# Two attention matmuls of a pair issued together, and the dense matmuls of both shares behind them

## The chip, the core and the metric

The kernel runs on one core of a Trainium2 chip. The core has a matrix engine (TensorE, PE in the profile, with its weight loads as PEld), a vector engine (VectorE, DVE), an activation engine (ScalarE, ACT), GpSimd (POOL), and a queue engine (SyncE, SP) that issues all the kernel's transfers. The metric is the device time of one execution in microseconds; the smaller the better.

## The reference

Two branches work on the same x (2048 rows, 512 columns, fp32) and are mixed by a gate per row:

```python
g = _sigmoid((x * gate_w).sum(-1, keepdims=True))
# A: a 2-D Fourier transform written as matrix products, real part only
a = x @ Wd_re.T;  b = x @ Wd_im.T
y = Ws_re @ a - Ws_im @ b
# B: attention with 32 heads of 16 columns, each query sees itself and the 255 keys before it
q, k, v = split(x @ wqkv)
p = softmax(where(mask, q @ k.T * 16 ** -0.5, -1e9))
o = (p @ v) @ wo
return g * y + (1 - g) * o
```

Inputs are fp32. The kernel keeps that precision by splitting each operand into a high and a low part and taking three products (hi*hi, hi*lo, lo*hi).

## The kernel before

**Attention.** The 32 heads are four groups (NG) of four pairs (NP) of two heads. Keys and queries are taken in 32 blocks of 64 (NB). A step n is one group and one block, 128 steps in all (N), and each step has four pairs p. For each pair there are two score matmuls:

- S, in `s_pair` (matmul at L319): 64 queries of two heads, zero-padded to a 128-wide stationary operand (`PAD[0, n]`), against a window of up to 320 keys in `ring[1]`. VectorE adds the mask and takes the row extreme (L321, which reads the bank), ScalarE takes the exp and the row sum (L324, which reads SBUF). S gives the maxima and sums only.
- T, in `t_pair` (matmul at L384): 64 keys of two heads (`PAD[1, n]`) against up to 320 queries in `ring[0]`, which gives the scores transposed. The row maxima are extra contraction rows of `ring[0]`, brought there by `m_rows` (L331 to L335 and two transfers). ScalarE takes the exp straight out of the bank (L385), GpSimd cuts the two corners of the window (L390, L394).

`pv` (L411) multiplies the transposed probabilities with v, for two steps at a time, on every odd step behind the third pair. T runs LAG = 18 steps behind S, so step n issues the S of block n and the T of block k = n - 18. Steps 0 to 17 have S alone, steps 18 to 127 both, steps 128 to 145 T alone. `make_pad` (L302 on ScalarE, L304 on VectorE) makes the padded operands of the next step behind pair 0.

**Banks.** S, T and the small transposes of `m_rows` and `l_rows` share one pool of four PSUM banks (`ps_a`), `pv` has two, the dense matmuls have two (`ps_d`).

**Dense work.** Everything else that TensorE does, all with 512 columns, is one generator, `dense()`: the projections for q, k (L238), v and the hidden transform (L260), then the transform along the sequence (L442), then the output (L604). Its `yield` stands behind every matmul. `fill(n)` takes matmuls from it by a quota, half a pair's rate at each call: 3.0 a pair before step 18, then 3.5, and 3.6 once the projections are done (`FILL_FIRST`, `FILL_PROJ`, `FILL_SEQ`). What is left of the generator when the loop ends runs alone.

**Who decides the order.** TensorE's instructions stay in the order of the program text. Those of VectorE, ScalarE and SP are placed by a scheduler when the kernel is built, so moving a line on TensorE can change the order in those queues as well. Each engine then works through its queue in that order.

The profile's L80 to L90 are the helpers that split an operand or a result into its high and low part, L55 the helper that issues a transfer.

Of the kernel before, what the change touches and what calls it, by code (L numbers as in the profile page):

```python
# [31 lines left out]
def fnet_window_mix(ctx: ExitStack, tc: tile.TileContext, xT, x, wqk, wv, wr, wi, cr, ci, wo, gw, out):  # L32
# [36 lines left out]
    @contextmanager  # L69
    def behind(*engines):  # L70
        with ExitStack() as es:
            for e in engines:
                if e in last:
                    es.enter_context(tc.issue_after(last[e]))
            yield
# [92 lines left out]
    def clear_rows(i, ss):  # L168
        nc.gpsimd.memset(f(ring[i][96:128, :, ss * 512:(ss + 1) * 512]), 0.0)
# [7 lines left out]
    def clear_pads():  # L177
        for t in vpad:
            nc.gpsimd.memset(t, 0.0)
        for t in pads[1]:  # L180
            nc.gpsimd.memset(f(t[96:128]), 1.0)
            for h in range(2):
                a = t[96:128, :, 64 * h:64 * h + 64]
                nc.vector.tensor_scalar(a, f(a), mrow[96:128, h:h + 1], None, op0=OP.mult)
# [108 lines left out]
    def make_pad(i, n):  # L293
        if not 0 <= n < NG * NB:
            return
        t = pads[i][n % NPAD]
        b = n % NB
        with behind(*(("act", "dve") if n < NPAD else ())):
            for h in range(2):
                src, dst = f(ring[i][:96, :, b * BQ:(b + 1) * BQ]), t[:96, :, 64 * h:64 * h + 64]  # L300
                if i and h:
                    nc.scalar.activation(dst, src, AF.Copy, scale=half[:96, h:h + 1])  # L302
                else:
                    nc.vector.tensor_scalar(dst, src, half[:96, h:h + 1], None, op0=OP.mult)  # L304
        PAD[i, n] = t
# [3 lines left out]
    def s_pair(n, p):  # L309
        j = n % NB  # L310
        u, jj = divmod(n, 8)
        if jj == 0 and p == 0:
            ML[u] = [at.tile([P, NP * 8], F32, name="nm"), at.tile([P, NP * 8], F32, name="l")]
        nm, l = ML[u]
        k0 = max(0, (j - 4) * BQ)
        w = (j + 1) * BQ - k0
        c = slice(p * 8 + jj, p * 8 + jj + 1)
        ps = ps_a.tile([P, 512], F32, name="s", tag="st")
        nc.tensor.matmul(ps[:, :w], PAD[0, n][:, p], ring[1][:, p, k0:k0 + w], start=True, stop=True)  # L319
        sm = at.tile([P, WIN], F32, name="sm", bufs=3)  # L320
        mark("dve", nc.vector.tensor_tensor_reduce(out=sm[:, :w], in0=ps[:, :w], in1=mask[:, WIN - w:],  # L321
                                                   scale=1.0, scalar=3e38, op0=OP.add, op1=OP.min,
                                                   accum_out=nm[:, c]))
        mark("act", nc.scalar.activation(sm[:, :w], sm[:, :w], AF.Exp, bias=nm[:, c], scale=-1.0,  # L324
                                         accum_out=l[:, c]))
# [31 lines left out]
    def v_load(n):  # L357
        if n >= NG * NB:
            return
        g, kb = divmod(n, NB)  # L360
        raw = at.tile([P, 4, 64], F32, name="vr")
        for h in range(2):
            ld(raw[64 * h:64 * h + 64].rearrange("r (c j) x -> r c j x", j=2),
               v_scr[kb // 4][:, :, h, g, :].rearrange("c (j r) x -> r c j x", r=64))
        VR[n] = raw

    def v_spread(n):
        if n >= NG * NB:
            return
        raw = VR.pop(n)  # L370
        v2 = vpad[n // 4 % 2]
        for h in range(2):
            r = slice(64 * h, 64 * h + 64)
            nc.gpsimd.tensor_copy(v2[r, :, :, 16 * h:16 * h + 16], raw[r].rearrange("r j (p d) -> r j p d", d=16))
        V2[n // 4] = v2

    def t_pair(n, p):
        q0 = n % NB * BQ
        w = min(WIN, S - q0)
        if p == 0:  # L380
            PT[n] = at.tile([P, NP, WIN], F32, name="pt", bufs=3)
        pt = PT[n]
        ps = ps_a.tile([P, 512], F32, name="t", tag="st")
        nc.tensor.matmul(ps[:, :w], PAD[1, n][:, p], ring[0][:, p, q0:q0 + w], start=True, stop=True)  # L384
        nc.scalar.activation(pt[:, p, :w], ps[:, :w], AF.Exp, scale=-1.0)  # L385
        if p % 2:
            ph = slice(p - 1, p + 1)
            for h in (0, 64):
                a = pt[h:h + 64, ph, 0:64]
                nc.gpsimd.affine_select(a, a, pattern=[[0, 2], [1, 64]], compare_op=OP.is_ge, fill=0.0,  # L390
                                        base=0, channel_multiplier=-1)
                if w == WIN:
                    a = pt[h:h + 64, ph, 256:320]
                    nc.gpsimd.affine_select(a, a, pattern=[[0, 2], [-1, 64]], compare_op=OP.is_gt, fill=0.0,  # L394
                                            base=0, channel_multiplier=1)

    def pv(n):
        g, kb = divmod(n, NB)
        v2 = V2[n // 4][:, n % 4]
        pt = PT.pop(n)  # L400
        q0 = kb * BQ
        w = min(WIN, S - q0)
        q = q0
        while q < q0 + w:
            sb = q // 512
            e = min(q0 + w, (sb + 1) * 512)
            first = (g, sb) not in OT
            if first:
                OT[g, sb] = ps_o.tile([P, 512], F32, name="o")
            for p in range(NP):  # L410
                nc.tensor.matmul(OT[g, sb][32 * p:32 * p + 32, q - sb * 512:e - sb * 512], v2[:, p],  # L411
                                 pt[:, p, q - q0:e - q0], start=first, stop=kb == 8 * sb + 7,
                                 skip_group_check=True)
            q = e
        if kb % 8 == 7:
            sb = kb // 8
            ps = OT.pop((g, sb))
            rl = at.tile([P, 512], F32, name="rl", bufs=1)
            ls = l_scr[g * 4 + sb]
            ld(rl, bass.AP(tensor=ls.tensor, offset=ls.offset, ap=[[512, 2 * NP], [0, 16], [1, 512]]))  # L420
            nc.vector.tensor_mul(rl, ps, rl)
            ld(o_scr[sb][g], rl)
# [190 lines left out]
    def need(key):  # L613
        while key not in have:
            next(stream)
# [3 lines left out]
    def ring_ahead(n):  # L619
        nonlocal loaded  # L620
        while loaded < 16:
            g, ss = divmod(loaded, 4)
            if n >= 32 * g + 8 * ss:
                need(("qk", g, ss))
            if ("qk", g, ss) not in have or n - LAG < 32 * (g - 1) + 8 * ss + 9:
                break
            with behind(*(("sp",) if g == 0 else ())):
                ring_load(g, ss)
            loaded += 1

    def fill(n):
        nonlocal quota
        rate = FILL_FIRST if n < LAG else FILL_SEQ if "proj" in have else FILL_PROJ
        quota += rate / 2
        while quota >= 1:
            next(stream, None)
            quota -= 1
# [7 lines left out]
    for n in range(N + LAG + 2):  # L645
        if n in (1, 3, 5):
            for i in range(2):
                clear_rows(1 - i, (n + 1) // 2)
        if n == 7:
            clear_pads()  # L650
        k = n - LAG
        ring_ahead(n + 1)
        if -4 <= k < N - 4 and k % 4 == 0:
            for c in range(2):
                need(("v", (k + 4) % NB // 2 + c))
            with behind(*(("sp",) if k < 4 else ())):
                v_load(k + 4)
        if -4 <= k and k % 4 == 2:
            v_spread(k + 2)
        if n == 0:  # L660
            make_pad(0, 0)
        if k == 0:
            make_pad(1, 0)
        for p in range(NP):
            if n < N:
                s_pair(n, p)
            fill(n)
            if 0 <= k < N:
                t_pair(k, p)
            if p == 0:  # L670
                make_pad(0, n + 1)
                if k >= 0:
                    make_pad(1, k + 1)
            fill(n)
            if p == 2 and n % 2:
                for j in (k - 2, k - 1):
                    if 0 <= j < N:
                        pv(j)
                if n % 8 == 1 and 1 < n <= N + 1:
                    m_rows(n // 8 - 1)  # L680
                    l_rows(n // 8 - 1)
# [47 lines left out]
```

## Time and profile before

| | us |
|---|---|
| median of 3 runs | 880.83 |
| lowest and highest run | 879.98, 882.15 |
| the profiled execution, its own time | 881.33 |
| its span | 879.5 |
| TensorE busy in the span | 866.5 |
| VectorE busy | 600.1 |
| ScalarE busy | 585.3 |
| GpSimd busy | 385.0 |

The span is the time from the first to the last instruction that the profiler recorded. Busy time of TensorE counts overlapping matmuls once. The first S and T that stand in one step start at 95.87 and 99.02, the last S at 668.6, the last T at 751.9; what follows is dense work and the output.

### The profile page before, as it was taken

The page shows a single profiled execution, that of the slowest core. Times are in us where ns is not written, and L with a number is a line of the kernel's source. Part 1 is how long each engine was busy: PE and PEld are TensorE (multiplying, and loading weights), DVE is VectorE, ACT ScalarE, POOL GpSimd, SP SyncE. Part 2 cuts the span into 40 slices and gives each one's busy share as a digit, 9 for nine tenths or more (in the row PEclk, how much of TensorE's full clock was granted, in tenths as well). Part 3 has the DMA queues.
Part 4 walks back from the last instruction along what each step waited for, and adds up shares of the span by engine and source line. Part 5 has one row for each costly group of instructions (what it writes and reads, how often), then busy time and mean ns, then how long its engine had stood idle before and what let it go on. Part 6 is the DMA issues. An engine that isn't in the chain of part 4 may idle for free.

```text
span 879.5 us, 17216 instructions
## 1 busy us (share of the span) xinstructions
PE 866.5 (99%) x5184; PEld 692.2 (79%) x5184; DVE 600.1 (68%) x1965; ACT 585.3 (67%) x1794; POOL 385.0 (44%) x1069
## 2 busy tenths in 40 slices
PE   7999899999999999999999999999999999999997
PEld 6888678777877878787778787877878777788885
DVE  4688788777887677777777777778776443454342
ACT  5488788889888887888878878888776444100010
POOL 9100165555544447564455566545656664000000
PEclk9999899999999999999999999999999999999999
DMA  7877668775766136543544353579643323455452
GB/s 265 261 228 214 198 205 272 233 237 174 221 207 210 45 99 200 147 138 120 175 131 140 127 148 115 143 230 348 211 143 126 130 92 126 137 174 156 149 159 88
DMA packets 89823, 152.13 MB, mean 173 GB/s; under 512 B 26753, under 2 KB 35457, under 8 KB 89729
## 3 DMA queue, kind: packets, MB, share of 16 engines
q1 hardware_dynamic: 89728, 151.02, 55.0%
q8 instruction: 41, 0.67, 0.3%
q14 instruction: 54, 0.43, 0.2%
HBM read 103.81 MB, written 47.19 MB: 172 GB/s over the span
## 4 chain that ended last, share of the span: by engine, by line
PE 98%; DMA 1%; ACT 1%; issue 0%; DVE 0%; SPq 0%; ACTq 0%
PE dc L442 41%; PE dab L260 10%; PE dqk L238 10%; PE s L319 9%; PE o L411 8%; PE t L384 8%; PE dv L260 5%; PE t L604 5%; PE s L226 1%; DMA ev<-o_scr 1%; PE s L343 0%; PE s L331 0%; DMA pt<-xT 0%; ACT sm L324 0%; ACT raw L80 0%
## 5 line engine op out<-in xcount | busy, mean ns | idle before, releaser
L442 PE MATMUL dc<-big,hi 128*128 128x512 f32 x1024 | 354.9, 395 | 0.0
L390 POOL TENSOR_SCALAR_AFFINE_SELECT pt<-pt 64x128 f32<-64x128 f32 x512 | 192.7, 376 | 292.1 <-ACT pt L385 276.2
L324 ACT ACTIVATE sm<-sm,nm 128x320 f32<-128x320 f32 (+4 forms) x512 | 276.8, 542 | 59.4 <-DVE nm L321 56.7
L321 DVE CUSTOM_DVE_ANT_0 sm<-s,mask 128x320 f32<-128x320 f32 (+4 forms) x512 | 232.3, 462 | 118.3 <-PE s L319 94.0
L385 ACT ACTIVATE pt<-t 128x320 f32<-128x320 f32 (+4 forms) x512 | 208.0, 412 | 81.3 <-PE t L384 78.7
L442 PEld LDWEIGHTS dc<-big,hi 128*128 128x128 f32 x1024 | 186.8, 188 | 28.0 <-issue 1.5
L442 PE MATMUL dc<-big,lo 128*128 128x512 f32 x512 | 202.6, 396 | 0.0
L319 PE MATMUL s<-ring,pad 128*128 128x320 f32 (+4 forms) x512 | 160.7, 314 | 0.0
L394 POOL TENSOR_SCALAR_AFFINE_SELECT pt<-pt 64x128 f32<-64x128 f32 x448 | 160.3, 358 | 0.0
L384 PE MATMUL t<-ring,pad 128*128 128x320 f32 (+4 forms) x512 | 154.8, 302 | 3.0 <-ACT pad L302 2.6
L304 DVE TENSOR_SCALAR pad<-ring,half 96x256 fp32r<-96x256 f32 x384 | 121.8, 359 | 19.7 <-PE t L384 19.2
L319 PEld LDWEIGHTS s<-ring,pad 128*128 128x128 f32 x512 | 96.4, 188 | 38.7 <-issue 9.3
L384 PEld LDWEIGHTS t<-ring,pad 128*128 128x128 f32 x512 | 96.5, 189 | 20.3 <-ACT pad L302 2.9
L442 PEld LDWEIGHTS dc<-big,lo 128*128 128x128 f32 x512 | 96.2, 188 | 16.5 <-issue 1.6
L83 DVE TENSOR_TENSOR lo<-raw,hi 128x512 fp32r<-128x512 f32 x146 | 100.0, 711 | 0.3 <-ACT hi L80 0.3
L324 ACT ACTIVATION_READ_ACCUMULATOR sm<-sm,nm 128x1 f32 x512 | 98.1, 192 | 0.0
L82 DVE CAST hi<-raw 128x512 fp32r<-128x512 f32 x142 | 56.8, 437 | 51.8 <-PE dc L442 31.8
L260 PE MATMUL dab<-hi,big 128*128 128x512 f32 x256 | 91.1, 396 | 0.0
L238 PE MATMUL dqk<-big,hi 128*128 128x512 f32 x240 | 87.3, 399 | 0.0
L80 ACT CAST raw<-ev 128x512 fp32r<-128x512 f32 x16 | 9.9, 622 | 110.0 <-DVE lo L83 72.3
L411 PE MATMUL o<-pt,vpad 128*32 128x320 f32 (+4 forms) x1408 | 78.6, 352 | 0.0
L411 PEld LDWEIGHTS o<-pt,vpad 128*32 128x32 f32 x1408 | 36.0, 109 | 36.9 <-issue 19.8
(79 smaller groups left out, 823.1 us busy)
## 6 DMA issues: line engine op xcount, KB each, us to landing
qk_scr<-hl SPq DMA_DIRECT2D x32, 512.0 KB
ring<-qk_scr SPq DMA_DIRECT2D x32, 512.0 KB
raw<-cr SPq DMA_DIRECT2D x32, 512.0 KB
raw<-ci SPq DMA_DIRECT2D x32, 512.0 KB
ab_scr<-hl SPq DMA_DIRECT2D x20, 512.0 KB
big<-ab_scr SPq DMA_DIRECT2D x20, 512.0 KB
ring<-qk_scr SPq DMA_DIRECT2D x32, 256.0 KB
r_scr<-ev SPq DMA_DIRECT2D x25, 256.0 KB
```

What stands on the lines that cost most here:

```text
L238: nc.tensor.matmul(ps, w[a][:, c:c + 128], XT[dk, ss][:, b], start=n == 0, stop=n == 11)
L260: nc.tensor.matmul(ps, XT[dk, ss][:, a, c * 128:(c + 1) * 128], wh[b], start=n == 0, stop=n == 11)
L304: nc.vector.tensor_scalar(dst, src, half[:96, h:h + 1], None, op0=OP.mult)
L319: nc.tensor.matmul(ps[:, :w], PAD[0, n][:, p], ring[1][:, p, k0:k0 + w], start=True, stop=True)
L321: mark("dve", nc.vector.tensor_tensor_reduce(out=sm[:, :w], in0=ps[:, :w], in1=mask[:, WIN - w:], scale=1.0, scalar=3e38, op0=OP.add, op1= ...
L324: mark("act", nc.scalar.activation(sm[:, :w], sm[:, :w], AF.Exp, bias=nm[:, c], scale=-1.0, accum_out=l[:, c]))
L384: nc.tensor.matmul(ps[:, :w], PAD[1, n][:, p], ring[0][:, p, q0:q0 + w], start=True, stop=True)
L385: nc.scalar.activation(pt[:, p, :w], ps[:, :w], AF.Exp, scale=-1.0)
L390: nc.gpsimd.affine_select(a, a, pattern=[[0, 2], [1, 64]], compare_op=OP.is_ge, fill=0.0, base=0, channel_multiplier=-1)
L394: nc.gpsimd.affine_select(a, a, pattern=[[0, 2], [-1, 64]], compare_op=OP.is_gt, fill=0.0, base=0, channel_multiplier=1)
L411: nc.tensor.matmul(OT[g, sb][32 * p:32 * p + 32, q - sb * 512:e - sb * 512], v2[:, p], pt[:, p, q - q0:e - q0], start=first, stop=kb == 8 ...
L442: nc.tensor.matmul(ps, w[a][:, s8 * 128:(s8 + 1) * 128], ab[SC[i]][:, b], start=i == 0 and a + b == 0, stop=i == 15 and a == 1)
```

## The change

In each pair the call `fill(n)` that stood between `s_pair` and `t_pair` moves behind `t_pair`. T of a pair is then issued directly behind S, and the two shares of dense matmuls stand behind them in one run; behind pair 0 the calls of `make_pad` stand between the two shares, as before.

```diff
--- before
+++ after
@@ -664,9 +664,9 @@
         for p in range(NP):
             if n < N:
                 s_pair(n, p)
-            fill(n)
             if 0 <= k < N:
                 t_pair(k, p)
+            fill(n)
             if p == 0:
                 make_pad(0, n + 1)
                 if k >= 0:
```

## The prediction

> **What bounds the kernel now.** I read the page first: engines, then the chain that ended last.
>
> ```profile
> PE 866.5 (99%) x5184; PEld 692.2 (79%) x5184; DVE 600.1 (68%) x1965; ACT 585.3 (67%) x1794; POOL 385.0 (44%) x1069
> PE 98%; DMA 1%; ACT 1%; issue 0%; DVE 0%; SPq 0%; ACTq 0%
> ```
>
> TensorE is the bound: 98% of the chain is its own work, so a reordering can only pay or cost through (a) the pace of the matmul stream and (b) TensorE's waits. For (b) the list of TensorE's waits has two entries that concern T:
>
> ```profile
> PE t L384 <- ACT pad L302: 2.6, 1, 2.6
> PE t L384 <- ACT pt L385: 0.4, 1, 0.4
> ```
>
> One long and one short wait in 512 T. For (a) the timeline in the middle of the attention loop:
>
> ```profile
> 306.56 0.31 PE L319 MATMUL s<-ring,pad 128*128 128x320 f32 x1
> 306.70 0.39 PE L260 MATMUL dab<-hi,big 128*128 128x512 f32 x1
> 306.93 0.31 PE L384 MATMUL t<-ring,pad 128*128 128x320 f32 x1
> 307.08 0.39 PE L260 MATMUL dab<-lo,big 128*128 128x512 f32 x1
> ```
>
> Columns: start in us, length, engine, line, operation. Lengths overlap; what counts is start to start. S (L319) is followed after 0.14 to 0.15 us, a dense matmul after 0.23, T (L384) after 0.15. Over all rows the medians are 147 ns behind a 320-column S, 147 behind such a T, 227 to 233 behind 512 columns. It makes no difference what follows: dense to dense has a median of 228 to 230, dense to S or T 229 to 231.
>
> **Part 1: the matmul stream.** Per pair the order S, 1 or 2 dense, T, 1 or 2 dense becomes S, T, 2 to 4 dense. The quota is added twice in both, so by the end of each pair the same dense matmuls have been issued (some 3.5 a pair), and the built order shows the same totals. S and T stand together in the 110 steps that have both: 440 pairs. Before step 18 there is no T and after step 127 no S; nothing changes there.
>
> The only new neighbourhood is T directly behind S. No row shows it, so I bound it by what T's weight load needs. Each weight load takes 188 ns in the record (PEld), longer than the 147 ns of the S that would cover it. How much must really be covered is shown where a matmul is very short:
>
> ```profile
> 426.70 0.19 PE L384 MATMUL t<-ring,pad 128*128 128x64 f32 x1
> 426.70 0.19 PEld L442 LDWEIGHTS dc<-big,hi 128*128 128x128 f32 x1
> 426.73 0.47 PE L442 MATMUL dc<-big,hi 128*128 128x512 f32 x1
> 427.04 0.40 PE L442 MATMUL dc<-big,lo 128*128 128x512 f32 x1
> ```
>
> The load starts with the 64-column T; the dense matmul behind it frees the array at 427.04, and less its usual 0.23 it had its weights at 426.81: about 0.11 us after the load began. So a load is hidden behind any matmul of 0.11 us or more, and S holds the array for 0.147. It already hides the load of a dense matmul, of the same 128x128 shape, 397 times. Estimate for T behind S: 147 ns, as now: sum 0. [...] The narrow S and T at the ends of a group expose the rest of a load before and after alike.
>
> [...]
>
> **Part 2: the first T.** At step 18 TensorE waits for the first T's padded operand:
>
> ```profile
> 95.87 0.31 PE L319 MATMUL s<-ring,pad 128*128 128x320 f32 x1
> 96.02 0.40 PE L238 MATMUL dqk<-big,hi 128*128 128x512 f32 x1
> 98.58 0.34 DVE L304 TENSOR_SCALAR pad<-ring,half 96x256 fp32r<-96x256 f32 x1
> 99.02 0.60 PE L384 MATMUL t<-ring,pad 128*128 128x320 f32 x1 [2.60 <-ACT pad L302]
> ```
>
> The table of stretches puts the granted clock at 0.50 from 98.25 to 105.07; the page's 0.97 of 50:150 is this. ScalarE's pads were done at 98.32, so what came last is VectorE's pad, at 98.92. In the built order the instructions ahead of that pad on VectorE are the same as before, and they need only the S of 95.87 and earlier matmuls. T therefore still starts at 99.0, but the one dense matmul that ran inside the gap is now behind T. Queued behind the waiting T is the whole matmul stream, and with it the evictions. Cost: one dense matmul that was free: +0.23 us at full clock, 0.43 at half if the half-clock stretch grew with it. I take 0.23, since the stretch ends at a time of its own.
>
> **Part 3: the banks.** S and T share four banks; VectorE (L321) frees S's, ScalarE (L385) frees T's. T is asked for 0.40 us earlier on average (the one or two dense matmuls it overtakes). Rhythm and distance between T's stay; the question is whether ScalarE's exp follows. I went through the timeline's T rows: from the exp of the T two pairs back to a T's start the median is 1.32 us, and 23 of 510 have under 0.5. If every exp stayed where it is in time while its T moved up, 16 T would wait, 1.3 us together. If it all moved up with T, 0. ScalarE has room: it waited for T 78.7 us in 119 waits, which an earlier T shortens; in the built order an exp of T no longer stands behind the exp of its own S (121 of 440 did, 1 does). In between I take half: +0.65 us. VectorE's order changes in places (an eviction ahead of an S), but S keeps its place; for its banks I take nothing, the cover being ScalarE's and VectorE's idle fifth; uncovered it is the second rival's kind of cost.
>
> The one recorded wait of a T for a bank:
>
> ```profile
> 177.27 0.60 ACT L86 ACTIVATE hl<-dab 128x512 fp32r<-128x512 f32 x1 [1.54 <-PE dab L260]
> 177.76 0.34 ACT L324 ACTIVATE sm<-sm,nm 128x64 f32<-128x64 f32 x1
> 178.09 0.42 ACT L385 ACTIVATE pt<-t 128x320 f32<-128x320 f32 x1
> 178.57 0.41 PE L384 MATMUL t<-ring,pad 128*128 128x320 f32 x1 [0.39 <-ACT pt L385]
> ```
>
> ScalarE works in order: an eviction that waited (its matmul was long done, so for its store's buffer) held up the exp. In the built order this exp stands ahead of the 0.34 us one: -0.2 us.
>
> **What else moves.** The pads for the next step are issued behind the first T; those after the first have 2.2 us and mostly 8 to 10 on ScalarE. GpSimd's order is unchanged and its input comes earlier. On SP some ring loads now stand ahead of the small row stores (l_scr, m_scr); those rows are read five steps, some 22 us, later. Sum 0. The final phase (745 us on) is untouched.
>
> **Sum.** +0.23 +0.65 -0.2 = +0.7 us on the profiled execution's 881.33 (span 879.5 and 1.8 around it): 882.0. That execution lies 0.5 above the median of the three runs, 880.83; against the median the forecast is 881.5. About 0.3%, 2.6 us, is what a measurement of this kernel can tell from no change, so this is "same".
>
> **Rivals.**
> - *ScalarE's exp comes later relative to where it was (slower).* If the exps slip by 0.1 us behind their present times while T is asked for 0.40 earlier, the shortfalls over the same rows add to 3.4 us; by 0.2, to 5.9. From about 0.07 on it is a measurable loss. For: ScalarE is 80 to 86% busy in 150 to 650. Against: its 78.7 us of waiting for T. At 0.1 that is 880.83+0.23-0.2+3.4 = 884.3. Chance 0.18.
> - *One new wait that halves the clock (slower).* The wait at 99.0 cost 2.8 us and then 6.83 us at clock 0.50, that is 3.4: 6.2 in all. One more, say a T behind a late pad or eviction, gives 880.8+6.2 = 887.0. Against: the longest other wait of a T in the trace is 0.39. Chance 0.08. [...]
> - *T's weight load is not hidden behind S (slower).* [...] Against: the 64-column row above. Chance 0.03.
> - *The waits shrink (faster).* The half-clock stretch is two stretches of 3.41; if it were one, -1.7 us; with the late starts of T outside the first (1.4 us in all, from the rows) gone, -3.1: 877.7. For: where the gap falls against those stretches may vary. Against: the gap gets longer. Chance 0.10.
> - *The edit does nothing in the stream* can be left out: the built order has the 440 adjacent pairs.
>
> **How the numbers follow.** Forecast (same): 0.61. Slower 0.18+0.08+0.03 = 0.29; faster 0.10. Range: down to 878.6, the lowest run (879.98) less the 1.4 us of small T waits; up to 886, which takes in the exp rival up to a slip of some 0.17 us and leaves out the two dearer ones.
>
> **What would show it.** Right: S to T 147 ns, TensorE still 98% of the chain, the first T again at 99.0 with a gap of 3.0 and half clock behind it, T waits for banks under 2 us. Wrong: S to T of 180 or more; many short waits "PE t <- ACT pt"; a second half-clock stretch.

## The result and the profile after

The changed kernel takes 882.54 us (median of 21 runs, 881.37 to 884.02), the kernel before 880.86 beside it (21 runs, 878.96 to 882.35). The ratio is 1.0018, 95% interval 1.0012 to 1.0024: 1.6 us slower, 1.1 to 2.1. This lies within the 0.3% that the prediction counted as "no change", but it is not zero. The profiled execution took 882.81 with a span of 881.0, that is 1.5 more than the profiled execution before.

From the page of the kernel after, busy time by engine and the chain by engine:

```profile
PE 867.3 (98%) x5184; PEld 690.6 (78%) x5184; DVE 604.8 (69%) x1965; ACT 590.3 (67%) x1794; POOL 384.9 (44%) x1069
PE 93%; DVE 2%; DMA 2%; ACT 1%; issue 0%; SPq 0%; ACTq 0%
```

TensorE's busy time has hardly moved (867.3 us against 866.5 before), yet its share of the chain fell from 98% to 93%: the chain now leaves TensorE for VectorE, ScalarE and transfers. The list of TensorE's waits (engine, operation, what it waited for; total us, times, longest) shows where:

```profile
PE t L384 <- ACT pad L302: 2.8, 1, 2.8
PE s L319 <- ACT pt L385: 0.8, 2, 0.6
PE t L384 <- ACT pt L385: 0.7, 2, 0.4
PE t L384 <- DVE nm L321: 0.2, 1, 0.2
PE dab L260 <- DVE hl L88: 0.2, 1, 0.2
```

One long wait as before, but T, S and a dense matmul now wait for banks: for VectorE's row extreme (`nm`, L321), for ScalarE's exp (`pt`, L385), for an eviction (`hl`, L88). The list holds the longer waits only; late starts of 0.05 to 0.15 us are found by going through the rows. The timeline of TensorE in the middle of the loop (start, length, engine, line, operation):

```profile
304.27 0.31 PE L319 MATMUL s<-ring,pad 128*128 128x320 f32 x1
304.43 0.31 PE L384 MATMUL t<-ring,pad 128*128 128x320 f32 x1
```

T starts 0.16 us behind S in this row, and over all rows the median from S to T is 147 ns: T's weight load, 0.19 us from 304.28 on in the row, is hidden behind S. Around the first T the timeline after reads:

```profile
96.23 0.31 PE L319 MATMUL s<-ring,pad 128*128 128x320 f32 x1
98.94 0.34 DVE L304 TENSOR_SCALAR pad<-ring,half 96x256 fp32r<-96x256 f32 x1
99.38 0.38 PE L384 MATMUL t<-ring,pad 128*128 128x320 f32 x1 [2.84 <-ACT pad L302]
99.60 0.39 PE L238 MATMUL dqk<-big,hi 128*128 128x512 f32 x1
```

T starts 3.15 us behind its S, as before (95.87 to 99.02), with the dense matmul now behind it instead of in the gap. Half clock follows, but shorter here; the table of stretches (window, its length, busy us of PE, PEld, DVE, ACT and POOL with counts, granted clock, DMA share, GB/s):

```profile
98.00:102.00 4.00, 2.62 (x10) 2.23 (x11) 2.97 (x8) 2.10 (x7) 0.55 (x2) 0.81 0.54 167
102.00:106.00 4.00, 4.00 (x17) 3.44 (x16) 1.99 (x8) 2.49 (x7) 1.45 (x5) 0.77 0.99 221
```

At half clock for x us of a 4 us window the mean is 1 - x/8; 0.81 and 0.77 give 1.5 and 1.8, together about 3.4 us; a window from 100.45 to 103.87 has 0.50. Before, it was 6.8. The same kernel profiled again had 6.8 (below), so this length is not fixed by the order, and the 1.7 us between the two is no work of the change.

The granted clock that is on record for each run says more. It is a mean over the span, rounded to 0.001. It is 1.000, hardly any half clock, in 28 of 80 runs of the kernel before (on four chips), but in 1 of 33 runs of the changed one. So half clock has become more frequent; that the longer gap is the reason is likely, not shown. It does not make up the difference: where the clock is 0.999 or more the changed kernel is 1.3 us slower in the means (33 and 7 runs), at 0.997 and 0.998 1.4 (36 and 16), below that 1.6 (11 and 10). Nor does a run get longer by all that half clock takes: the kernel before has means of 880.5, 881.2 and 880.9 in these three classes. What takes it up the record doesn't show.

A bank wait in full, all engines, after:

```profile
169.62 0.68 DVE L90 SCALAR_TENSOR_TENSOR hl<-dab,hl 128x512 fp32r<-128x512 f32 x1
170.22 0.47 DVE L321 CUSTOM_DVE_ANT_0 sm<-s,mask 128x320 f32<-128x320 f32 x1
170.24 0.31 PE L319 MATMUL s<-ring,pad 128*128 128x320 f32 x1
170.63 0.07 DVE L321 DVE_READ_ACCUMULATOR2_ANT nm<- 128x1 f32 x1
170.76 0.19 PEld L384 LDWEIGHTS t<-ring,pad 128*128 128x128 f32 x1 [0.56 <-DVE nm L321]
170.76 0.42 PE L384 MATMUL t<-ring,pad 128*128 128x320 f32 x1 [0.21 <-DVE nm L321]
```

T's bank was that of the S one pair earlier, and is free when VectorE has read it (170.22 to 170.7). VectorE got to it only then because it had a 0.68 us eviction to do first. Behind S, T could have started at 170.24 + 0.147 = 170.39; it started at 170.76, and its weight load, which also waited, ran uncovered. In rows like these the T that waited gives way after 0.25 us (170.76 to 171.01) and not after 0.147: the bare load took 0.107 on top of the wait. From that follows an estimate of the slack: behind a 320-column matmul (0.147) a bank may become free some 0.04 us after that matmul's start before it costs, and behind a dense one (0.23) some 0.12. The change moved T from behind a dense matmul to behind a 320-column one.

### The profile page after: what moved, and what is told of

It reads as the page before. It is cut to its first block, busy times and chain, and to the rows that moved or that the text cites. A ratio compares the mean times of both kernels' runs of the same rounds, so it can differ in the third digit from the quotient of the medians.

```text
span 881.0 us, 17206 instructions
## 1 busy us (share of the span) xinstructions
PE 867.3 (98%) x5184; PEld 690.6 (78%) x5184; DVE 604.8 (69%) x1965; ACT 590.3 (67%) x1794; POOL 384.9 (44%) x1069
## 4 chain that ended last, share of the span: by engine, by line
PE 93%; DVE 2%; DMA 2%; ACT 1%; issue 0%; SPq 0%; ACTq 0%
PE dc L442 40%; PE s L319 9%; PE dab L260 9%; PE t L384 8%; PE dqk L238 8%; PE o L411 8%; PE t L604 5%; PE dv L260 5%; DMA qk_scr<-hl 1%; DMA pt<-xT 1%; DMA ab_scr<-hl 1%; DVE sm L321 1%; ACT sm L324 0%; PE s L343 0%; PE s L331 0%
## 5 line engine op out<-in xcount | busy, mean ns | idle before, releaser
L442 PE MATMUL dc<-big,hi 128*128 128x512 f32 x1024 | 341.0, 394 | 0.0
L321 DVE CUSTOM_DVE_ANT_0 sm<-s,mask 128x320 f32<-128x320 f32 (+4 forms) x512 | 232.6, 462 | 114.6 <-PE t L384 74.9
L385 ACT ACTIVATE pt<-t 128x320 f32<-128x320 f32 (+4 forms) x512 | 210.8, 414 | 117.9 <-PE t L384 114.4
L442 PEld LDWEIGHTS dc<-big,hi 128*128 128x128 f32 x1024 | 189.4, 188 | 28.1
L384 PE MATMUL t<-ring,pad 128*128 128x320 f32 (+4 forms) x512 | 158.3, 309 | 3.8 <-ACT pad L302 2.8
L260 PE MATMUL dab<-hi,big 128*128 128x512 f32 x256 | 86.6, 395 | 0.2 <-DVE hl L88 0.2
L238 PE MATMUL dqk<-big,hi 128*128 128x512 f32 x240 | 84.2, 398 | 0.0
```

Source lines behind the costliest of these rows:

```text
L238: nc.tensor.matmul(ps, w[a][:, c:c + 128], XT[dk, ss][:, b], start=n == 0, stop=n == 11)
L260: nc.tensor.matmul(ps, XT[dk, ss][:, a, c * 128:(c + 1) * 128], wh[b], start=n == 0, stop=n == 11)
L442: nc.tensor.matmul(ps, w[a][:, s8 * 128:(s8 + 1) * 128], ab[SC[i]][:, b], start=i == 0 and a + b == 0, stop=i == 15 and a == 1)
```

## The experiments

Four explanations of the 1.6 us stood against each other. *Bank theory*: T, asked for earlier, meets banks that VectorE and ScalarE free late, in the steps where dense evictions are many. *Pace theory*: two adjacent 320-column matmuls cost a few ns more a pair, everywhere. *First-T theory*: the dense matmul put behind the long gap. *Chance*: waits that move between executions. "Before" and "after" below are the two kernels; ratios are to before, run on the same chip.

**Which steps.** One half of the loop gets the new order, the other keeps the old. The edit is to the changed kernel.

```diff
             if n < N:
                 s_pair(n, p)
+            together = n < 64      # second kernel: n >= 64
+            if not together:
+                fill(n)
             if 0 <= k < N:
                 t_pair(k, p)
-            fill(n)
+            if together:
+                fill(n)
```

> The change for steps below 64 alone (184 of the 440 adjacent pairs, all of them beside the projections). Bank theory (T asks for its PSUM bank earlier than ScalarE and VectorE free one, and a weight load that has waited is not covered): nearly the whole cost is here, late starts of S and T at a bank of about 3.6 us in all against 1.4 before, time +1.0 to +1.7 us on the kernel before. Pace theory (each T right behind an S costs 3 to 4 ns more, wherever it is): 184 x 3.7 ns = +0.7 us, and late starts at banks as before. First-T theory (one dense matmul leaves the gap at the first T): +0.23 and nothing else.

> The change for steps 64 and later alone (256 adjacent pairs beside the sequence transform). Bank theory: late starts at banks stay at 1.4 us, time within 0.3 us of the kernel before. Pace theory: S of step 127 has moved by 256 x 3.7 ns = 0.95 us against S of step 64, time +0.9. First-T theory: 0.

New order in steps below 64 only: 883.17 beside 881.08, ratio 1.0025 (1.0014 to 1.0036), +2.2 us, more than any of the theories expected. From 64 on only: 880.13, ratio 0.9993 (0.9985 to 1.0001), -0.6. The sum is +1.6, as for the whole change. All of the measurable cost lies in the first half. The pace theory has a trace all the same: with the new order in steps 64 to 127, S of step 127 stands 0.92 to 0.98 us later against S of step 64 than before (after, its repeat, the late half, and three kernels below), and -0.03 with the old order there. That is some 3.7 ns for each of the 256 pairs. In the late half's profile 0.45 of its 0.92 is gone again when the output stage begins, and that stage no longer waits for its last load (1.4 us in the profile before, 0 here), which can take up the rest, though no run tests that; what gives the 0.45 back I could not tell.

**The same kernel again.**

> The changed kernel itself, once more, for a second profile. Bank theory: the same late starts at the same steps (21, 31, 33, 45), 3 to 4 us in all. If these were chance of one execution, they lie elsewhere or are gone. The half-clock stretch behind the first T may be 3.4 or 6.8 us long, and the last load of the output may or may not hold TensorE: if both vary here, the profiled difference of 1.5 us between the two kernels held 3.6 us of chance.

881.92 (12 runs), ratio 1.0015 (1.0007 to 1.0024). The late starts at banks repeat to about 0.03 us in the two profiles of this kernel, at the same T. The last column has three more profiles with the new order in these steps (the early half, and two kernels below):

| T, counted singly from 0, and its place | bank freed by | late, us, in both profiles | in the three others |
|---|---|---|---|
| 25, at 133 us | VectorE | 0.25 to 0.27 | 0.23 to 0.27 |
| 26, at 134 us | VectorE | 0.05 to 0.06 | 0.04 to 0.06 |
| 37, at 148 us | VectorE | 0.11 to 0.12 | 0.12 to 0.14 |
| 54, at 170 us | VectorE | 0.45 to 0.48 | 0.06 to 0.08 |
| 107, at 240 us | ScalarE | 0.15 | 0.14 to 0.15 |
| 109, at 243 us | ScalarE | 0.53 | 0.53 to 0.54 |

Together 1.57 us: VectorE's 0.89, ScalarE's 0.68. With T 54 as in the three others it is 1.2, of which VectorE's is 0.5. T 54's large wait is thus no fixed part of the change; in the early half, whose steps up to there have the same order, the reduce ends 0.06 us behind the start of the S (170.58) that T 54 follows:

```profile
170.56 0.08 DVE L321 DVE_READ_ACCUMULATOR2_ANT nm<- 128x1 f32 x1
170.73 0.39 PE L384 MATMUL t<-ring,pad 128*128 128x320 f32 x1
```

One dense matmul waits for an eviction by VectorE at 265.7, 0.37, in all five profiles. Against that, four late starts of the old order (three S, one T: 0.12, 0.10, 0.135, 0.24, together 0.60, at the same places in most profiles of it) are gone. Net +1.0, or +0.6 with the smaller T 54, and the dense 0.4. The largest one freed by ScalarE, from the timeline of the repeat:

```profile
242.18 0.41 ACT L385 ACTIVATE pt<-t 128x320 f32<-128x320 f32 x1
242.65 0.41 PE L384 MATMUL t<-ring,pad 128*128 128x320 f32 x1 [0.27 <-ACT pt L385]
```

The exp that empties the bank, that of the T one pair earlier, ends at 242.59, and T follows at once. What did not repeat: the half-clock stretch (3.4 in after, 6.8 here), the lateness at 114 to 118 us behind an eviction that waited for its store (0.91 in after, 0 here, 1.85 in the late half), and the wait of a T near 178 (0.72 before, 0.65 after, 0 here).

**T ahead of S.** If closeness alone made the waits, S would inherit them. The edit is to the changed kernel.

```diff
-            if n < N:
-                s_pair(n, p)
             if 0 <= k < N:
                 t_pair(k, p)
+            if n < N:
+                s_pair(n, p)
             fill(n)
```

> T ahead of S in each pair, both adjacent, both dense shares behind. If it is the closeness of two bank requests that costs, late starts at banks of about 3.6 us as in the changed kernel, now at S as well as at T, and time +1 to +2 us on the kernel before. If it is only that T asks earlier relative to its own exp, S is the one that has moved (0.15 us later) and the waits fall back towards 1.4 us and the time to within 0.5 us of before. Pace theory: S behind T costs the same 3 to 4 ns, +1.6 us.

881.62, ratio 1.0002 (0.9993 to 1.0011). The late starts add to 4.0 us, and now most are of S, which is the second of the two: the waits fall mostly on the matmul that stands second. But the time is that of before. This order also moves the first T ahead of the S of its step, and its half-clock stretch was the short one, so the run does not price the bank waits. Still, 4.0 us of late starts beside +0.2 us of time count against taking the late starts one for one as time. Inconclusive on the time.

**The first T.** The padded operand of the first T is made two steps earlier, in the old and in the new order.

```diff
-        if k == 0:
+        if k == -2:
             make_pad(1, 0)
```

> The kernel before with the first padded operand of T made two steps earlier (step 16 in place of 18). The first T then finds its operand ready: the gap of 2.8 us and the half-clock stretch behind it (1.7 or 3.4 us) should go, -4.5 to -6 us on the kernel before. If the first T waits for something else as well (its transfers, a bank), part of the gap stays and the clock still falls.

> The same on the changed kernel: -4.5 to -6 us on the changed kernel. First-T theory (the change costs because a dense matmul leaves the gap and the gap lengthens): without the gap the difference to e5 is under 0.3 us less than the 1.5 us between changed and before; bank theory: the difference to e5 stays at 1.3 to 1.7 us.

Old order: 879.63 beside 881.11, ratio 0.9991 (0.9983 to 1.0000), far from the gain expected. New order: 881.14, ratio 1.0002 (0.9993 to 1.0011). With no gap at the first T in either, the difference between the orders is 1.5 us in the medians and 0.8 in the means, and the noise of these 12 and 11 runs leaves from about 0 to 2. So it probably stays, and the first T is then not the main part of what the change costs, but the pair does not show this clear of noise. The missing gain shows in the timeline of the old order: S of step 20 stands 5.77 us earlier, and 14 us later

```profile
113.03 0.60 ACT L86 ACTIVATE hl<-dqk 128x512 fp32r<-128x512 f32 x1 [3.53 <-DMA qk_scr<-hl]
113.53 0.43 ACT L385 ACTIVATE pt<-t 128x320 f32<-128x320 f32 x1
114.01 0.41 PE L384 MATMUL t<-ring,pad 128*128 128x320 f32 x1 [2.26 <-ACT pt L385]
```

an eviction waits 3.53 us on ScalarE for the store of its buffer (`hl`, two buffers) to land, the exp behind it is late, and T waits for the bank. By step 64 some 3.7 of the 5.8 us are given back: work that came earlier ran into the transfers, whose share in the table of stretches is 1.06 to 1.08 from 102 to 114 us (the DMA engines fully busy). The granted clock halves again from 114.7, for 3.41 us (0.59 in the mean of 114 to 118).

**Fewer banks.** Three instead of four, in both orders: if waits for banks are the price, it must grow.

```diff
-    ps_a = ctx.enter_context(tc.tile_pool(name="ps_a", bufs=4, space=PSUM))
+    ps_a = ctx.enter_context(tc.tile_pool(name="ps_a", bufs=3, space=PSUM))
```

> The kernel before with three PSUM banks in place of four for S and T. Every S and T then needs a bank freed one request earlier. Bank theory: many late starts at banks, several tens of us. Rivals (pace, first T): no difference to the other order.

> The changed kernel with three banks. Bank theory (two requests back to back want two free banks at once): clearly slower than e7, by over 10 us, where the difference was 1.5 us with four banks. If banks are not what the change costs, the difference to e7 stays at 1 to 2 us.

Old order 893.28 (ratio 1.0146, 1.0131 to 1.0160; several tens of us were expected), new order 899.69 (1.0213, 1.0200 to 1.0226). The new order now costs 6.4 us, four times 1.6, though less than the over 10 expected. The rows have 58 late starts of S and T (14.6 us) in the old order and 66 (18.7) in the new. Their difference, 4.1, with 3.7 ns for each of the 440 pairs and the first T's 0.2 makes 5.9 (an estimate). Neither profile has half clock behind the first T (over the spans the clock is 1.000 and 0.999; one stretch of 3.41 us would make it 0.998), so that this pair is free of it. The line that grew most in the lists of TensorE's waits is T waiting for VectorE; old order, then new order:

```profile
PE t L384 <- DVE nm L321: 0.7, 2, 0.5
```

```profile
PE t L384 <- DVE nm L321: 3.2, 9, 0.6
```

This supports the bank theory, with VectorE as the engine that frees too late more often; the run changes the whole rhythm, so it shows the direction and not the size at four banks.

**Room for the evictions.** To stop the waits for stores, `hl` gets a third buffer, paid for by the buffers of the output stage, with the early pad in both orders.

```diff
-    ev = ctx.enter_context(tc.tile_pool(name="ev", bufs=5))
+    ev = ctx.enter_context(tc.tile_pool(name="ev", bufs=3))
...
-        hl = ev.tile([P, 2, 512], F32R, name="hl", bufs=2)
+        hl = ev.tile([P, 2, 512], F32R, name="hl", bufs=3)
```

> Kernel before with the early first pad, three buffers in place of two for the split results that wait for their store (hl), and three in place of five for the other results (ev), to make room. If ScalarE's wait for a store near 109 to 113 us gave back what the early pad won, it is gone: -4.5 to -6 us on the kernel before. If the stores are late because the transfers are behind (they are busy 99% there), the wait only moves: -1.5 to -2.5 us, as with e5. Fewer ev buffers may cost some us in the later stage.

> The same on the changed kernel. Bank theory: the late starts at banks that repeat in every profile of the changed order (T of 133, 148, 170, 240, 243 us, 1.5 us in all) don't come from the stores and stay, so 1 to 1.7 us over e9. If what the change costs is the ScalarE queue held up by stores, the difference to e9 is under 0.5 us.

893.96 (1.0152, 1.0136 to 1.0168) and 893.72 (1.0150, 1.0133 to 1.0167): by their profiles they lost some 15 and 12 us behind the last S, mostly in the output stage, which waits for its buffers (10.0 us in 8 waits and 8.4 in 6), and that hides any difference in the total. Inside the loop the two differ as elsewhere: S of step 127 stands 2.94 us earlier than before in the old order, 0.75 in the new, a difference of 2.2 us. In the new order the T of the table wait as above, T 54 only 0.06. As a measurement of time the pair failed.

**VectorE's gate work left out.** This kernel, made from the changed one, omits the products of the gate (16 instructions on VectorE) and uses logits of zero.

```diff
-        t = GX[tb // 2][:, HALVES[tb % 2]]
-        nc.vector.scalar_tensor_tensor(t, t, 1.0, gwb, op0=OP.mult, op1=OP.mult,
-                                       accum_out=gl[:, tb:tb + 1])
+        if tb == 0:
+            nc.gpsimd.memset(gl, 0.0)
```

> The changed kernel without the gate's products on VectorE (L203; the gate's logits are left out and set to 0, all else stays). Theory that S's banks come free late because VectorE has other work ahead of the reduce: the late start of T at 170 us (0.45 us, released by the reduce of the S before it) goes or shrinks to under 0.15, the one at 133 us (behind a split and a pad) stays, time -0.3 to -1 us on the changed kernel. If the reduce's own length sets it, both stay.

The four late T that VectorE frees are gone, the one at 133 too, which was expected to stay, and the two that ScalarE frees stay (0.15 and 0.54). But two other T now wait for VectorE, 0.64 at 143.5 and 0.46 at 145.0, for banks of the small transposes of `l_rows` and `m_rows`. Yet the time rose to 885.85, ratio 1.007 (1.005 to 1.009); the gain expected was missed. The timeline (its line numbers are lower by 1 past the edit):

```profile
155.19 0.60 ACT L86 ACTIVATE hl<-dab 128x512 fp32r<-128x512 f32 x1 [4.36 <-DMA ab_scr<-hl]
156.23 0.43 ACT L384 ACTIVATE pt<-t 128x320 f32<-128x320 f32 x1
```

Without the products the loads of x behind them go out earlier, and an eviction waits 4.36 us for its store; the exp and a T come late, and half clock follows for 3.41 us (0.57 in the mean of 156 to 160). So the run shows that these waits hang on what stands in VectorE's queue, and says nothing of their price.

**A faster version.** The old order with the early pad, three `hl` buffers, and four buffers for the output stage; the gate's weights share one of those to make the room.

```diff
-    ev = ctx.enter_context(tc.tile_pool(name="ev", bufs=5))
+    ev = ctx.enter_context(tc.tile_pool(name="ev", bufs=4))
...
-            ld(gwb, bass.AP(tensor=gw.tensor, offset=gw.offset, ap=[[0, P], [1, D]]))
+            GW.append(ev.tile([P, D], F32, name="ev"))
+            ld(GW[0], bass.AP(tensor=gw.tensor, offset=gw.offset, ap=[[0, P], [1, D]]))
...
-        hl = ev.tile([P, 2, 512], F32R, name="hl", bufs=2)
+        hl = ev.tile([P, 2, 512], F32R, name="hl", bufs=3)
...
-        if k == 0:
+        if k == -2:
             make_pad(1, 0)
```

> Kernel before with the early first pad and three hl buffers, four ev buffers (the gate's weights take one of them while the gate is made, in place of a tile of their own). In e9 S of step 127 was 3.4 us earlier than before, of which the first 17 steps had lost 1.7, and the output with three ev buffers lost 15. If four ev buffers are enough: 4 to 5 us faster than the kernel before. If the output stage needs all five: slower by up to 10 us.

876.25 beside 880.89, ratio 0.9949 (0.9937 to 0.9961): 4.5 us faster than before, as expected, and faster than after by more. (The expectation's 3.4 and 1.7 us are by another reading; the two profiles give 2.9 for S of step 127 and 2.2 for the first 17 steps.) Its stretch where the first T stood still:

```profile
98.00:102.00 4.00, 4.00 (x22) 3.42 (x21) 4.00 (x14) 3.79 (x12) 3.35 (x6) 1.00 0.60 196
102.00:106.00 4.00, 4.00 (x26) 2.69 (x25) 3.12 (x13) 3.76 (x13) 1.80 (x7) 1.00 1.05 218
```

TensorE is busy throughout at full clock. The 6.2 us that the prediction counted at the first T (2.8 of waiting, 3.4 of clock) can mostly be had, once the waits for stores that take their place are removed too.

## Why the prediction was right, and where it was off

Forecast 881.5 in 878.6 to 886.0, likeliest case "same"; measured 882.54, +1.6 us for a predicted +0.7. The case was right. One cost was put at nothing and is not, one was no term at all, and one term has the right size by luck.

- **Stream, T behind S: sum 0.** The main part was right: 147 ns. A load that shows by 41 ns (188 less 147) in each of the 440 pairs, 18 us, is excluded: the load starts with S and T follows at 147. The 64-column row, with its estimate that 0.11 us must be covered, was the right one to read. What was missed is the few ns a pair, 0.95 us over the second half by the rows, none of it visible in that half's time; at the same rate the 184 pairs below step 64 would make 0.7 (an estimate).
- **First T: +0.23.** Right by the rows, though no run times it alone. At equal half-clock length S of step 20 against step 17 stands later by 0.28 us (the repeat) and 0.23 (the early half) than before. The gap grew, T's start behind its S didn't, and the stretch after it ended at a time of its own, as assumed: half clock stood from 98.25 to 105.07 before and from 100.45 to 103.87 after.
- **ScalarE's banks: +0.65.** Right in size, 0.68, but by luck: in two late starts and not in 16 small ones, and both wait for the exp of the T one pair earlier, where the prediction had looked at the T two pairs back.
- **VectorE's banks: "I take nothing".** This is the step that failed. VectorE's late releases cost 0.89 us on T (0.5 where T 54 is hardly late) and 0.37 on a dense matmul. Two things were wrong in it. T does not always take over the bank of a T: already in the trace before, of the 384 T that need no new pad (pairs 1 to 3 of a step) 109 wait, by their semaphores, for VectorE alone and not for ScalarE. And VectorE's idle fifth was taken as cover, but idle time over a stage is no cover for one bank: a single eviction of 0.68 us ahead of the reduce was enough. The rows searched were those of T behind exps alone. The same search for T behind reduces would have found half of it: in the profile before, the reduces in question ended 0.21 us ahead of T 26 and 0.13 ahead of T 54, less than the 0.40 by which T moved, but 0.75 ahead of T 25 and 1.08 ahead of T 37. There VectorE itself comes later; at T 37 it has an eviction ahead of the reduce (147.41), which before stood behind it (147.73). The old order's small waits (0.60), which vanish, were not counted either.
- **T at 178: -0.2.** Not shown. That wait hangs on a store's landing and is 0.72 before, 0.65 after, 0.93 in the late half (old order there) and 0 in the repeat.
- **Rivals.** The exps did not slip; the clock rival did not occur in after; the load rival is excluded; one half-clock stretch of 3.41 us instead of two did occur in the profiled run, but not in the repeat (6.8).
- **Signs.** S to T of 147 ns and the gap at the first T came as said, T's waits for banks stayed under 2 us; TensorE's share of the chain did not stay at 98% (93).

Below step 64 the rows' terms, 0.25 + 1.0 + 0.4 + 0.7, make 2.3 us, and 1.9 with T 54 as in the early half's own profile, beside +2.2 (1.2 to 3.2) measured for that half alone. That the sum meets the time does not prove each term: the 0.7 is an estimate, and T ahead of S had more late starts at hardly any time. For the second half rows (+0.5 by the start of the output) and time (-0.6, up to +0.1) do not quite meet; that stays open. The one profiled pair would have misled: its +1.5 us holds a half-clock stretch shorter by chance (-1.7), a lateness at 115 (+0.9) that the repeat has not, and a wait for the output's last load that took up what came late (-1.4).

## What to carry to other kernels

Before two matmuls are put side by side, look up who empties the bank of the second, and what that engine has queued just ahead of the release: behind a short matmul there was some 0.04 us of slack, behind a long one 0.12 (estimates from the rows), and a mean of idle time says nothing of it. Profile more than once, and a variant too: five of six late starts repeated to some 0.05 us in five profiles, the sixth was 0.45 or more in two and under 0.1 in three, and waits behind a store's landing come and go by 1 to 2 us. A gap that is closed gives its time back unless the next limit, here the evictions' buffers, is moved with it (0.9991 of the time with the gap closed, 0.9949 with the buffers too).

## What the runs showed of the hardware that I had not expected

- A TensorE wait of 2.26 us (at 114.0, early pad, old order) and one of 2.20 (at 156.7, no gate) were followed by half clock for 3.41 us; one of 1.58 (at 117.5, late half) was not (1.00 from 114 to 122). The same gap at the first T was followed by 3.41 us in after and in the late half, by 6.83 before and in the repeat, and in the two with three banks (TensorE waits of 2.6 and 2.8 us) by none.
- A T that waited for its bank loaded its weights only then: the two start together (at 170.76 in after, at 133.65 and 242.65 in the repeat), and the next matmul follows after 0.25 us in place of 0.147, 0.107 on top of the wait.
- Two adjacent 320-column matmuls cost some 3.7 ns a pair more than two that stand apart (0.92 to 0.98 us over 256 pairs), by the rows of steps 64 to 127; the time of that half does not show it.
